# Linear attention and a maxout FFN on one core: a PSUM bank for each pair's small products, a late stage for left queries, and new numbers for the order

## The chip, the cores and the metric

The kernel runs on one core of a Trainium2 chip. The metric is device time in microseconds, from the first to the last instruction with what lies around them; before the change it is 717.27 us, the median of three runs (717.15 to 717.32).

## The reference

Attention without a softmax over scores: q is normalized by exp over the head dimension, k over the sequence, and `kv` is a 64 x 64 matrix per head. Its output x, 4608 rows of 512, goes through a maxout layer of three weights and a last product.

```python
batch, n_heads, seq, head_dim = 8, 8, 576, 64      # fp32
q_s = exp(q - max(q, -1));  q_s = q_s / (sum(q_s, -1) + 1e-9)
k_s = exp(k - max(k, 2));   k_s = k_s / (sum(k_s, 2) + 1e-9)
kv = einsum('bhsd,bhse->bhde', k_s, v)
x = einsum('bhsd,bhde->bhse', q_s, kv)             # to (4608, 512)
h = maximum(maximum(x @ w1, x @ w2), x @ w3)       # 512 -> 768
out = h @ w_out                                    # 768 -> 512
```

## The kernel before

**Tiles.** Two heads form a pair, so a batch has four pairs and the kernel 32 of them, numbered n = 4 b + g. The 576 rows of a head are 512 main rows and 64 left rows. The main rows of a batch are one chunk of the FFN; the left rows of all eight batches, 8 x 64 = 512, are a ninth, last chunk. x lies with its features on partitions, in `xbuf` for main rows and in `left` for left ones.

**FFN.** Each fp32 operand is split into a high and a low part in fp32r, and each product is three matmuls (low x high, high x low, high x high). A chunk has 18 gate groups of 12 matmuls (`gate`, L693) and 4 groups y of 18 (`second`, L732), all 128 x 512: 288 a chunk, 2592 in all. They are called main products here, and they accumulate in the four banks of the PSUM pool `pf`. Their weights are made on the core in 24 slices (18 of w1 to w3, 6 of w_out): a slice is loaded into a buffer `wst`, its words are joined in `wx` (L342 to L355), and it is split into `wh` and `wl`, or `oh` and `ol` (L363, L370). Buffers are few (`ROOMS`), and the loads wait for them on SP.

**Attention.** Batches 0 and 1 are "turned" (`TURNED = 2`), to fill the start. For such a pair PE transposes k (L441 the main rows, L445 the left rows), DVE takes the maximum over the sequence (L450 to L452), ACT the exp into `keT` (L456, L457), PE transposes it back (L464, L466), ten small matmuls form kv (L511), and ACT scales it into the block-diagonal `bdf` (L527). q is reduced on DVE (L550), goes through exp on ACT in ten pieces of 64 columns where `Q_BY_ACT` says so (L567), is scaled (L595), transposed on PE (L636, left L640), copied to `qf` (L645, L647) and multiplied with `bdf` in full fp32 (L663, once for 512 columns and once for 64). ACT and DVE split the result into `x`, or `left` (L666, L668). From batch 2 on, in the 24 "plain" pairs, q and k are not transposed by PE; the x product is three fp32r matmuls for the 512 main columns and, some products later, three for the 64 left ones.

**PSUM.** Eight banks: four of `pf`, three of `pa` for what is 512 wide, and one, `ps`, for everything small of all pairs. Its four quarters are handed out in turn (`next(small)`): left part of k, left part of keT, kv, left part of q, left x.

**What sets the order.** The order on every engine is written by a planner (`Streams`) while the program is built: each step has a cost, events it waits for, rooms in pools that it takes and frees, and a rank. Ranks come from numbers: `AT` and `STEP` for the eight turned pairs, `FIRST` and `CHUNK` for the plain ones, `SLICES_AT`, `SLICE` and `SLICE_STEP` for weight slices, `GATES_AT` for main products, and the string `FIRST_LOADS` for the loads of batch 0 on SP (lower case main rows, upper case left rows, w a weight slice). On the chip an engine runs its rows in that order and waits in place.

```python
quarters = ps.tile([P, 4, P], F32, name="ps")
small = (quarters[:, i % 4, :] for i in itertools.count())
```

Of the kernel before, what the change touches and what calls it, by code (L numbers as in the profile page):

```python
# [37 lines left out]
SLICES_AT, SLICE_STEP, SLICE_HI, SLICE_LO = -30.5, 2.83, 6.78, 0.26  # L38
GATES_AT = 50.0
FIRST_LOADS = 'qwQKkKqvVvwQkkwqVkwqvv'  # L40
ROOMS = 3, 2, 3, 4

Q_BY_ACT = (0, 1, 2, 3, 4, 5, 6)
# [6 lines left out]
def dve_reduce(n):  # L50
    return (n + 140) / 960
# [28 lines left out]
class Streams:  # L80
# [88 lines left out]
    def issue(self, t, e, c, s):  # L169
        step = s[4]  # L170
        end = t + c
# [24 lines left out]
def linear_attention_then_maxout_ffn(  # L196
# [26 lines left out]
    nc = tc.nc  # L223
# [22 lines left out]
    pa = ctx.enter_context(tc.tile_pool(name="pa", bufs=3, space=PSUM))  # L246
    ps = ctx.enter_context(tc.tile_pool(name="ps", bufs=1, space=PSUM))
# [16 lines left out]
    q0 = early.tile([P, H, 5, D], F32, name="q0")  # L264
    v0 = early.tile([P, H, 5, D], F32, name="v0")
    bdf = [start.tile([P, P], F32, name=f"bdf{i}", bufs=1) for i in range(2)]
    qbuf = [start.tile([P, 2, 5, D], F32, name=f"q1{i}", bufs=1) for i in range(2)]
# [14 lines left out]
    nc.gpsimd.memset(q0[LEFT:P, :, 4, :], 0.0)  # L282
    for i in range(2):
        nc.gpsimd.memset(bdf[i], 0.0)
    for i in range(2):
        nc.gpsimd.memset(qbuf[i][LEFT:P, :, 4, :], 0.0)
        nc.gpsimd.memset(vbuf[i][:, :, :, D:NV], 1.0)
        nc.gpsimd.memset(vbuf[i][LEFT:P, :, 4, :], 0.0)
# [13 lines left out]
    st = Streams({"pf": 4, "pa": 3, "ps": 4, "keT": 1, "hp": NJ, "tmp": 3, "ke": 2, "qe": 2, "qf": 1, "qt": 2, "tb": 1, "qT": 2, "qhl": 1}, {"pf": in_pf})  # L302
    late_pools, turn_pools = [], []

    quarters = ps.tile([P, 4, P], F32, name="ps")
    small = (quarters[:, i % 4, :] for i in itertools.count())
# [67 lines left out]
    class Pair:  # L374


        def __init__(self, b, g):
            self.b, self.g = b, g
            self.hs = slice(2 * g, 2 * g + 2)
            self.n = b * NP + g  # L380
            self.m = self.n % 2
            self.turned = b < TURNED
            if b == 0:
                self.kt, self.vt, self.qt = k0[:, :, self.hs], v0[:, self.hs], q0[:, self.hs]
            else:
                self.kt, self.vt = kbuf[self.m], vbuf[self.m]
                if self.turned:
                    self.kt = self.kt.rearrange("p h s d -> p (h s d)").rearrange("p (s h d) -> p s h d", s=5, h=2)

        def ago(self, what, *u):  # L390

            return (what, self.n - 2, *u) if self.n >= 2 else None

# [15 lines left out]
        def v_load(self):  # L409
            if self.b:  # L410
                prev = self.ago("kv") if self.n >= NP + 2 else None
                for hh in range(2):
                    yield Step("S", 0.64, [prev], kb=200)
                    nc.sync.dma_start(out=self.vt[:, hh, 0:4, 0:D], in_=head_rows(v, self.b, 2 * self.g + hh))
# [3 lines left out]
        def q_load(self):  # L418
            if self.b == 0:
                return  # L420
            if self.turned:
                prev = self.ago("qsub") if self.n >= NP + 2 else None
                self.qt = qbuf[self.m]
                yield Step("S", 0.64, [prev], kb=256)
                nc.sync.dma_start(out=self.qt[:, :, 0:4, :], in_=main_rows(q, self.b, self.hs))
                yield Step("S", 0.64, gives=("q", self.n), kb=50)
                nc.sync.dma_start(out=self.qt[0:LEFT, :, 4, :], in_=left_rows(q, self.b, self.hs))
# [6 lines left out]
        def k_turned(self):  # L434

            n, kt = self.n, self.kt
            rooms = [("pa", ("kT", n)), ("ps", ("kTl", n))]
# [6 lines left out]
            kTl = next(small)  # L444
            nc.tensor.transpose(  # L445
                out=kTl[:, :LEFT], in_=kt[:LEFT, 4].rearrange("p h d -> p (h d)"), identity=ident[:LEFT, :LEFT]
            )
            yield Step("V", dve_reduce(CH) + dve_reduce(LEFT) + 0.13)
            km = att.tile([P, 2], F32, name="km2", bufs=4)
            nc.vector.tensor_reduce(out=km[:, 0:1], in_=kT, op=ALU.max, axis=AX.X, negate=True)  # L450
            nc.vector.tensor_reduce(out=km[:, 1:2], in_=kTl[:, :LEFT], op=ALU.max, axis=AX.X, negate=True)
            nc.vector.tensor_tensor(out=km[:, 0:1], in0=km[:, 0:1], in1=km[:, 1:2], op=ALU.min)  # L452
            yield Step("A", act(CH) + act(LEFT) + 0.2, free=rooms)
            keT = start.tile([P, S], F32, name="keT", bufs=1)
            ks = self.ks = att.tile([P, 2], F32, name="ks", bufs=4)
            nc.scalar.activation(out=keT[:, :CH], in_=kT, func=AF.Exp, bias=km[:, 0:1], accum_out=ks[:, 0:1])  # L456
            nc.scalar.activation(  # L457
                out=keT[:, CH:], in_=kTl[:, :LEFT], func=AF.Exp, bias=km[:, 0:1], accum_out=ks[:, 1:2]
            )
            rooms = [("pa", ("ke", n)), ("ps", ("kel", n))]  # L460
            yield Step("T", 0.6, take=rooms + [("ke", n)], free=[("keT", n)])
            kep = pa.tile([P, CH], F32, name="pa")
            for s in range(4):
                nc.tensor.transpose(out=kep[:, s * P : (s + 1) * P], in_=keT[:, s * P : (s + 1) * P], identity=ident)  # L464
            kel = next(small)
            nc.tensor.transpose(out=kel[:LEFT, :], in_=keT[:, CH:], identity=ident)  # L466
            e = yield Step("AV", (act(CH) + act(P), dve(CH) + dve(P)), free=rooms)
            ke = self.ke = att.tile([P, 5, 2, D], F32, name="ke")
            for o, i in (
                (ke[:, 0:4].rearrange("p s h d -> p (s h d)"), kep),  # L470
                (ke[:LEFT, 4].rearrange("p h d -> p (h d)"), kel[:LEFT, :]),
            ):
                (nc.scalar.copy if e == "A" else nc.vector.tensor_copy)(out=o, in_=i)
# [24 lines left out]
        def k_steps(self):  # L498
# [3 lines left out]
            last = [("ps", ("kv", n))]  # L502
            yield Step(
                "T", 0.9, [("v", n), self.ago("xmm", 0), self.ago("xmm", 1)], take=last, free=[("ke", n)], gives=("kv", n)
            )
            kv = next(small)
# [17 lines left out]
            yield Step("A", 0.65, free=last if turned else (), gives=("bd", n) if turned else None)  # L524
            for r in heads:
                to = (bdf if turned else bdh)[self.m]
                nc.scalar.activation(out=to[r, r], in_=kv[r, 0:D], func=AF.Copy, scale=rk[r])  # L527
            if not turned:
                yield Step("V", 0.45, free=last, gives=("bd", n))
# [11 lines left out]
        def q_steps(self):  # L541
            n = self.n
            rows = 10 if self.turned else QS
            by_act = n in Q_BY_ACT
            qm = att.tile([P, rows], F32, name=f"qm{rows}", bufs=4)
            qs = att.tile([P, rows], F32, name=f"qs{rows}", bufs=4)
            yield Step("V", dve_reduce(rows * D), [("q", n)])
            if self.turned:
# [4 lines left out]
                if by_act:  # L553
                    yield Step("A", 5 * 0.33, take=[("qe", n)])
# [4 lines left out]
                qe = self.qe = start.tile([P, 5, 2, D], F32, name="qe", bufs=2)  # L559
                rows3 = qe.rearrange("p s h d -> p (s h) d")  # L560
                sums = qs.rearrange("p (s h) -> p s h", h=2)
                if by_act:
                    for hh in range(2):
                        if hh:
                            yield Step("A", 5 * 0.33, gives=("qsub", n))
                        for s in range(5):
                            nc.scalar.activation(  # L567
                                out=qe[:, s, hh, :], in_=src[:, hh, s, :], func=AF.Exp,
                                bias=qm[:, 5 * hh + s : 5 * hh + s + 1], accum_out=sums[:, s, hh : hh + 1],
                            )  # L570
                else:
# [3 lines left out]
                        in1=qm.rearrange("p (h s) -> p h s", h=2).unsqueeze(3).broadcast_to([P, 2, 5, D]),  # L575
                        op=ALU.subtract,
                    )
            else:
# [5 lines left out]
                )  # L584
            if not by_act:
# [4 lines left out]
            yield Step("V", 0.34)  # L590
# [34 lines left out]
        def x_place(self, u):  # L625
            if u == 0:
                return tuple(xbuf[self.b % 2][:, i, self.g, :] for i in range(2))
            return tuple(left[:, i, self.g, self.b * LEFT : (self.b + 1) * LEFT] for i in range(2))

        def turned_steps(self):  # L630

            n = self.n
            yield Step("T", 0.5, [("qn", n)], take=[("qf", n), ("pa", ("qT", n)), ("ps", ("qTl", n))], free=[("qe", n)])
            qT = pa.tile([P, CH], F32, name="pa")
            for s in range(4):
# [3 lines left out]
            qTl = next(small)  # L639
            nc.tensor.transpose(  # L640
                out=qTl[:, :LEFT], in_=self.qe[:LEFT, 4].rearrange("p h d -> p (h d)"), identity=ident[:LEFT, :LEFT]
            )
            e = yield Step("AV", (act(CH), dve(CH)), free=[("pa", ("qT", n))])
            qf = start.tile([P, S], F32, name="qf", bufs=1)
            (nc.scalar.copy if e == "A" else nc.vector.tensor_copy)(out=qf[:, :CH], in_=qT)  # L645
            yield Step("A", act(LEFT), free=[("ps", ("qTl", n))], gives=("qhl", n))
            nc.scalar.copy(out=qf[:, CH:], in_=qTl[:, :LEFT])  # L647
            self.terms = [(bdf[self.m], qf)]

        def x_steps(self, u):  # L650
            n, b = self.n, self.b
            cs = (slice(0, CH), slice(CH, S))[u]
            w = cs.stop - cs.start
            room = ("ps" if u else "pa", ("x", u, n))
            cost = f32(w) if self.turned else 3 * f32r(w)
            after = [("bd", n), ("qhl", n), ("xmm", n, 0) if u else None]
            if u == 0:
                after += [("gates", b - 2) if b >= 2 else None, "late" if b == 1 else None]
            yield Step("T", cost, after, take=[room], gives=("xmm", n, u), free=[("qf" if self.turned else "qhl", n)] if u else ())
            xT = (next(small) if u else pa.tile([P, CH], F32, name="pa"))[:, :w]  # L660
            last = len(self.terms) - 1
            for i, (l, r) in enumerate(self.terms):
                nc.tensor.matmul(out=xT, lhsT=l, rhs=r[:, cs], start=(i == 0), stop=(i == last))  # L663
            h, lo = self.x_place(u)
            yield Step("A", act(w))
            nc.scalar.copy(out=h, in_=xT)  # L666
# [257 lines left out]
```

## Time and profile before

| | us |
|---|---|
| median of three runs | 717.27 |
| the profiled execution | 717.27 |
| its span | 715.5 |
| PE busy | 685.4 |
| DVE busy | 401.7 |
| ACT busy | 254.0 |
| GpSimd busy | 55.1 |

How to read the lines of the profile: `L663 PE MATMUL pa<-qf,bdf` is line 663 of the kernel on TensorE, what it writes, and from what. A row of the timeline starts with its start and its length in us; `x2` counts instructions merged into the row; brackets hold the idle time of the engine before it and what ended it. A row of the waits reads: who waited, for whom, us in total, how often, the longest. A group of instructions gives its count, busy time and mean in ns, then the idle time before. PE's ends are modelled, and its instructions overlap, so the pace of a series is read from the starts. The program's fp32 matmuls appear as two rows each.

### The profile page before, as it was taken

How to read it: one execution, taken by the hardware profiler on the slowest of the kernel's cores; microseconds unless marked ns; L12 is line 12 of the kernel's file. 1: busy time of each engine (PE TensorE's matmuls, PEld its weight loads, DVE VectorE, ACT ScalarE, POOL GpSimd, SP SyncE). 2: the span in 40 equal slices, each digit the busy share in tenths (PEclk: the TensorE clock that was granted, in tenths of full speed). 3: DMA queues.
4: the chain of work that ended last, by engine and by line, in shares of the span. 5: the costliest groups of instructions: out<-in, count | busy, mean ns of one | idle time of the engine just before them, and what ended most of it. 6: DMA issues, size and time to landing. Idle time of an engine off the chain costs nothing.

```text
span 715.5 us, 9842 instructions
## 1 busy us (share of the span) xinstructions
PE 685.4 (96%) x3528; PEld 552.0 (77%) x3528; DVE 401.7 (56%) x812; ACT 254.0 (36%) x605; POOL 55.1 (8%) x69
## 2 busy tenths in 40 slices
PE   3779899999999999999999999999999999999997
PEld 2457687787888787888888888888888888888885
DVE  6789867388977977865477646653422112211220
ACT  4899745433443425422442234223411111111111
POOL 1222233100010000000000000000000000000000
PEclk9999999999999999999999999999999999999999
DMA  8947423315454334520253015200200010010002
GB/s 222 252 135 231 127 83 106 109 34 129 113 163 122 83 80 110 151 65 17 73 150 86 16 49 164 64 16 28 82 1 0 16 45 0 1 44 16 1 0 60
DMA packets 86417, 58.07 MB, mean 81 GB/s; under 512 B 53344, under 2 KB 77920, under 8 KB 86368
## 3 DMA queue, kind: packets, MB, share of 16 engines
q1 hardware_dynamic: 86288, 57.31, 28.9%
q8 instruction: 28, 0.46, 0.3%
q14 instruction: 21, 0.17, 0.1%
q10 hardware_dynamic: 80, 0.13, 0.0%
HBM read 40.89 MB, written 9.44 MB: 70 GB/s over the span
## 4 chain that ended last, share of the span: by engine, by line
PE 88%; ACT 4%; DVE 4%; DMA 2%; issue 1%; SPq 1%; DVEq 0%; ACTq 0%
PE pf L693 59%; PE pf L732 21%; PE ps L511 3%; PE pa L663 2%; ACT qe L567 2%; PE ps L663 1%; DMA wst<-in_moe_w_dram 1%; ACT keT L456 1%; ACT wst L359 0%; PE pa L464 0%; DMA v<-in_v_dram 0%; DVE m L705 0%; DVE wx L346 0%; PE pa L441 0%; DMA vt<-in_v_dram 0%
## 5 line engine op out<-in xcount | busy, mean ns | idle before, releaser
L693 PE MATMUL pf<-x,wh 128*128 128x512 f32 x1152 | 357.3, 391 | 0.0
L693 PEld LDWEIGHTS pf<-x,wh 128*128 128x128 f32 x1152 | 217.3, 189 | 47.0 <-issue 1.0
L693 PE MATMUL pf<-x,wl 128*128 128x512 f32 x576 | 231.1, 401 | 0.0
L705 DVE TENSOR_TENSOR m<-pf,m 128x512 f32<-128x512 f32 x108 | 74.4, 689 | 180.0 <-PE pf L693 177.5
L693 PEld LDWEIGHTS pf<-x,wl 128*128 128x128 f32 x576 | 108.7, 189 | 23.9 <-issue 0.7
L708 ACT CAST h_h<-m 128x512 fp32r<-128x512 f32 x54 | 33.6, 622 | 191.6 <-DVE m L705 191.4
L732 PE MATMUL pf<-ol,h_h 128*128 128x512 f32 x216 | 88.0, 408 | 0.1
L732 PE MATMUL pf<-oh,h_l 128*128 128x512 f32 x216 | 84.5, 391 | 0.0
L732 PE MATMUL pf<-oh,h_h 128*128 128x512 f32 x216 | 84.3, 390 | 0.0
L702 ACT COPY m<-pf 128x512 f32<-128x512 f32 x54 | 31.7, 587 | 57.8 <-PE pf L693 57.7
L732 PEld LDWEIGHTS pf<-ol,h_h 128*128 128x128 f32 x216 | 40.6, 188 | 9.2 <-DVE ol L370 0.7
L712 DVE TENSOR_TENSOR h_l<-m,h_h 128x512 fp32r<-128x512 f32 x54 | 36.9, 683 | 19.1 <-ACT h_h L708 19.0
L732 PEld LDWEIGHTS pf<-oh,h_l 128*128 128x128 f32 x216 | 40.5, 188 | 9.1
L732 PEld LDWEIGHTS pf<-oh,h_h 128*128 128x128 f32 x216 | 40.6, 188 | 7.6
L693 PE MATMUL pf<-left,wh 128*128 128x512 f32 x144 | 44.4, 389 | 0.0
L486 POOL PARTITION_ALL_REDUCE kma<-km x24 | 18.7, 779 | 299.7 <-DVE ke L489 146.8
L750 ACT COPY m<-pf 128x512 f32<-128x512 f32 x35 | 20.4, 587 | 59.8 <-PE pf L732 54.3
L355 POOL TENSOR_TENSOR wst<-wx,wst 128x512 int32<-128x512 int32 x24 | 31.6, 1318 | 90.9 <-DVE wx L351 55.5
L668 DVE TENSOR_TENSOR x<-pa,x 128x512 fp32r<-128x512 f32 x32 | 22.1, 689 | 29.4 <-ACT x L666 29.3
L600 DVE STREAM_TRANSPOSE tb<-qt 128x576 f32<-128x576 f32 x24 | 30.8, 1282 | 2.4 <-DMA qT<-tb 2.1
L666 ACT CAST x<-pa 128x512 fp32r<-128x512 f32 x32 | 18.7, 585 | 36.1 <-PE pa L663 36.1
L693 PEld LDWEIGHTS pf<-left,wh 128*128 128x128 f32 x144 | 27.0, 188 | 5.7
(114 smaller groups left out, 679.2 us busy)
## 6 DMA issues: line engine op xcount, KB each, us to landing
wst<-in_moe_w_dram SPq DMA_DIRECT2D x18, 512.0 KB, 5.0
out_dram<-m SPq DMA_DIRECT2D x32, 256.0 KB, 2.4
vt<-in_v_dram SPq DMA_DIRECT2D x56, 128.0 KB, 3.0
qt<-in_q_dram SPq DMA_DIRECT2D x24, 288.0 KB, 3.1
qT<-tb SPq DMA_DIRECT2D x192, 36.0 KB, 1.9
kt<-in_k_dram SPq DMA_DIRECT2D x24, 256.0 KB, 3.0
wst<-in_moe_w_out_dram SPq DMA_DIRECT2D x6, 512.0 KB, 3.3
q<-in_q_dram SPq DMA_DIRECT2D x8, 256.0 KB, 4.6
```

The source lines that it names most:

```text
L355: nc.gpsimd.tensor_add(out=low.bitcast(I32), in0=x.bitcast(I32), in1=low.bitcast(I32))
L511: nc.tensor.matmul(out=kv[r, :nv], lhsT=ke[rows, s, hh, :], rhs=self.vt[rows, hh, s, 0:nv], start=(s == 0), stop=(s == 4),)
L600: nc.vector.transpose(out=tb.rearrange("p e (c s) -> p s e c", s=QS), in_=self.qt.rearrange("p s (e c) -> p s e c", e=2))
L663: nc.tensor.matmul(out=xT, lhsT=l, rhs=r[:, cs], start=(i == 0), stop=(i == last))
L668: nc.vector.tensor_sub(out=lo, in0=xT, in1=h.bitcast(F32))
L693: nc.tensor.matmul(out=ps, lhsT=l[:, cc, js], rhs=r, start=(cc == 0 and t == 0), stop=(cc == NC - 1 and t == 2))
L702: nc.scalar.copy(out=m, in_=self.m.pop((j, 0)))
L705: nc.vector.tensor_max(out=m, in0=self.m.pop((j, i)), in1=m)
L708: nc.scalar.copy(out=h, in_=m)
L712: unit[e].tensor_sub(out=lo, in0=m, in1=h.bitcast(F32))
L732: nc.tensor.matmul(out=po, lhsT=l, rhs=r[:, j, :], start=(j == 0 and i == 0), stop=(j == NJ - 1 and i == 2))
L750: nc.scalar.copy(out=o, in_=po)
```

## The change

**A bank per pair.** The bank `ps` is gone. A pair's small products now lie in one bank that the pair takes for itself: left k in the first quarter, left keT in the second, kv in the third, a new sum of q in the fourth. The four pairs of batch 0 take their banks from `pf`, ahead of the first gate group; later pairs share a new pool `sm` with one bank (`BANKS = 3, 1`), held from the pair's first small product to its last.

**Left queries.** The 64 left rows of q of batches 0 and 1 are left out of the turned pairs, whose q is now 512 wide (`q0`, `q1`, `qe` with 4 instead of 5 parts). A stage `left_queries` does both batches at once after the turned part: two loads, six rows on DVE, exp and two copies on ACT, four transposes and eight products of 64 columns on PE. For it `bdf` keeps the matrices of all eight turned pairs.

**Left products.** In the plain pairs the three 64-column products stand between the three 512-column ones, in one step.

**Two kinds of q.** `Q_BY_ACT` now names pairs 0 and 3 to 7: eight pieces each. Pair 2 goes through one wide exp. Pair 1 (`Q_AFTER`) too, and isn't scaled before its product: with q transposed as weights, PE forms x in rows and the sums of q beside it (`of_head`, a matrix of ones per head), DVE divides, and PE transposes x back.

**Order.** All numbers of the order are replaced, and the planner takes PE's costs 1.85 times as high before 34 us of its own clock (`COLD`).

```diff
-FIRST, CHUNK, SLICE = 21.0, 39.5, 0.35
-AT = (16.0, 6.9, 25.7, 26.2, 99.1, 87.2, 114.2, 74.5)
-STEP = (0.38, 3.02)
-GATES_AT = 50.0
-FIRST_LOADS = 'qwQKkKqvVvwQkkwqVkwqvv'
+COLD = 34.0, 1.85
+FIRST, CHUNK, SLICE = 143.0, 39.5, 1.32
+AT = (38.7, -49.7, 32.6, 13.7, 143.7, 146.4, 163.0, 85.8)
+STEP = (7.87, 0.38)
+GATES_AT = 1000.0
+FIRST_LOADS = 'vkwkKqvwKVwVqqkwvqkv'
+BANKS = 3, 1
-Q_BY_ACT = (0, 1, 2, 3, 4, 5, 6)
+Q_BY_ACT = (0, 3, 4, 5, 6, 7)
+Q_AFTER = (1,)
...
-    ps = ctx.enter_context(tc.tile_pool(name="ps", bufs=1, space=PSUM))
+    sm = ctx.enter_context(tc.tile_pool(name="sm", bufs=BANKS[1], space=PSUM))
...
-    in_pf = []
+    in_pf = [("sm", n) for n in range(NP)]
...
+        def small_room(self):
+            return ("pf", ("sm", self.n)) if self.b == 0 else ("sm", self.n)
+        def take_small(self):
+            self.sm = (pf if self.b == 0 else sm).tile([P, CH], F32, name="pf" if self.b == 0 else "sm")
...
-            yield Step("T", 0.6, [("k", n)], take=rooms + [("keT", n)], gives=("ksub", n))
-            kT = pa.tile([P, CH], F32, name="pa")
+            yield Step("T", 0.6, [("k", n)], take=[*room, ("keT", n), self.small_room()], gives=("ksub", n))
+            self.take_small()
+            kT, kTl = pa.tile([P, CH], F32, name="pa"), self.sm[:, 0:LEFT]
...
-            kv = next(small)
+            if not turned:
+                self.take_small()
+            kv = self.sm[:, 2 * P : 3 * P]
...
-                        for s in range(5):
+                        for s in range(4):
                             nc.scalar.activation(
...
+            if self.after:
+                yield Step("A", act(rows * D), gives=("qn", n))
+                nc.scalar.activation(out=rows3, in_=rows3, func=AF.Exp)
+                return
...
+            for s in range(4):
+                l = qf[:, s * P : (s + 1) * P]
+                nc.tensor.matmul(out=sums[:, 2 * s : 2 * s + 2], lhsT=l, rhs=of_head, start=True, stop=True)
+                nc.tensor.matmul(out=xn[:, s * P : (s + 1) * P], lhsT=l, rhs=bdf[:, n], start=True, stop=True)
...
-            for i, (l, r) in enumerate(self.terms):
-                nc.tensor.matmul(out=xT, lhsT=l, rhs=r[:, cs], start=(i == 0), stop=(i == last))
+                parts = [(xT, slice(0, CH))] + ([] if self.turned else [(self.sm[:, 0:LEFT], slice(CH, S))])
+                last = len(self.terms) - 1
+                for i, (l, r) in enumerate(self.terms):
+                    for out, cs in parts:
+                        nc.tensor.matmul(out=out, lhsT=l, rhs=r[:, cs], start=(i == 0), stop=(i == last))
...
+            yield Step("V", dve(LEFT), free=[self.small_room()], gives=("xl", b, self.g))
+            nc.vector.tensor_sub(out=lo, in0=self.sm[:, 0:LEFT], in1=h.bitcast(F32))
+    def left_queries():
...
+        for g in range(NP):
             nc.tensor.transpose(
+                out=qTp[:, g * P : (g + 1) * P], in_=ql[:, 2 * g : 2 * g + 2].rearrange("p r d -> p (r d)"), identity=ident
             )
...
+        for n in range(TURNED * NP):
+            b, g = divmod(n, NP)
+            at = g * P + b * LEFT
+            nc.tensor.matmul(out=xT[:, at : at + LEFT], lhsT=bdf[:, n], rhs=qT[:, at : at + LEFT], start=True, stop=True)
```

Three places of the order, before and after. The first is ACT between the third and the fourth x of batch 0 (`CAST x`). Before:

```order
L666 CAST x_86<-pa 128x512
L666 CAST left<-ps 128x64
L527 ACTIVATE bdf_101<-ps,rk 64x64 x2
L456 ACTIVATE keT,ks<-pa,km_603 128x512
L457 ACTIVATE keT,ks<-ps,km_603 128x64
L645 COPY qf<-pa 128x512
L359 ACTIVATE wst<-wst 128x512
L342 ACTIVATE wx<-wst 128x512
L363 CAST wh_80<-wx 128x4x128
L647 COPY qf<-ps 128x64
L567 ACTIVATE qe,qs_144<-q_103,qm_143 128x64 x5
L359 ACTIVATE wst<-wst 128x512
```

And now:

```order
L693 CAST x_86<-pa 128x512
L466 ACTIVATE keT,ks<-pa,km_559 128x512
L467 ACTIVATE keT,ks<-sm,km_559 128x64
L649 COPY qf<-pa 128x512
L535 ACTIVATE bdf<-pf,rk 64x64 x2
L367 CAST wh_80<-wx 128x4x128
L363 ACTIVATE wst<-wst 128x512
L576 ACTIVATE qe,qs_138<-q_101,qm_137 128x64 x4
L693 CAST x_86<-pa 128x512
```

The copies of left columns are gone from between, and four instead of five pieces of exp (those of a pair of batch 1) stand ahead of the fourth x. From the program's start to that x, ACT has 112 rows before, with 50 such pieces, and 79 now, with 20.

The second place is PE around the last x product of batch 0. Before it stands among other turned steps, ahead of main product 34 to 36:

```order
L466 MATMUL ps<-ident,keT 64x128
L693 MATMUL pf<-x_86,wl_82 128x512
L693 MATMUL pf<-x_86,wh_79 128x512 x2
L693 MATMUL pf<-x_86,wl_83 128x512
L693 MATMUL pf<-x_86,wh_80 128x512 x2
L693 MATMUL pf<-x_86,wl_84 128x512
L693 MATMUL pf<-x_86,wh_81 128x512 x2
L663 MATMUL pa<-qf,bdf_101 128x512
```

Now it stands behind main product 21:

```order
L645 MATMUL pa<-ident,qe 128x128 x4
L472 MATMUL pa<-ident,keT 128x128 x4
L473 MATMUL sm<-ident,keT 64x128
L775 MATMUL pf<-x_86,wl_82 128x512
L775 MATMUL pf<-x_86,wh_79 128x512 x2
L690 MATMUL pa<-qf,bdf 128x512
L519 MATMUL sm<-vt_92,ke 64x64 x10
L775 MATMUL pf<-x_86,wl_82 128x512
```

Behind it the turned steps of batch 1 stand one by one among 12 to 33 main products, and the last turned x product has 261 main products ahead of it; before, the last one has 315, and its left part 321, and nine turned products and transposes of batch 1 stand in one row behind main product 96.

The third place is PE in a plain pair (b = 2). Before, six main products lie between the x product and its left part, and kv of the next pair follows after six more:

```order
L663 MATMUL pa<-q_l,bdh_1505 128x512
L663 MATMUL pa<-q_h,bdl_1509 128x512
L663 MATMUL pa<-q_h,bdh_1505 128x512
L693 MATMUL pf<-x_765,wl_84 128x512
L693 MATMUL pf<-x_765,wh_81 128x512 x2
L693 MATMUL pf<-x_765,wl_82 128x512
L693 MATMUL pf<-x_765,wh_79 128x512 x2
L663 MATMUL ps<-q_l,bdh_1505 128x64
L663 MATMUL ps<-q_h,bdl_1509 128x64
L663 MATMUL ps<-q_h,bdh_1505 128x64
```

Now the left products alternate with the others, and kv (L519) follows after 18 main products:

```order
L690 MATMUL pa<-q_l,bdh_1378 128x512
L690 MATMUL sm<-q_l,bdh_1378 128x64
L690 MATMUL pa<-q_h,bdl_1382 128x512
L690 MATMUL sm<-q_h,bdl_1382 128x64
L690 MATMUL pa<-q_h,bdh_1378 128x512
L690 MATMUL sm<-q_h,bdh_1378 128x64
L775 MATMUL pf<-x_665,wl_84 128x512
L775 MATMUL pf<-x_665,wh_81 128x512 x2
```

More of the change, by code (lines that the diff above doesn't have):

```diff
@@ L1 @@
-import itertools
 from contextlib import ExitStack
@@ L170, in issue @@
         step = s[4]
+        if e == "T" and t < COLD[0]:
+            c *= COLD[1]
         end = t + c
@@ L281, in linear_attention_then_maxout_ffn @@
         )
[L282 to L288, printed above, removed]
+    nc.gpsimd.memset(of_head, 0.0)
+    for h, r in enumerate(heads):
+        nc.gpsimd.memset(of_head[r, h : h + 1], 1.0)
+    nc.gpsimd.memset(bdf, 0.0)
     def main_rows(src, b, hs):
@@ L501, in k_steps @@
             ke = self.ke
-            last = [("ps", ("kv", n))]
+            after = turned and n in Q_AFTER
             yield Step(
-                "T", 0.9, [("v", n), self.ago("xmm", 0), self.ago("xmm", 1)], take=last, free=[("ke", n)], gives=("kv", n)
-            )
-            kv = next(small)
+                "T", 0.9, [("v", n), None if turned else self.ago("xmm")], take=() if turned else [self.small_room()],
+                free=[("ke", n)], gives=("kv", n),
+            )
+            if not turned:
+                self.take_small()
+            kv = self.sm[:, 2 * P : 3 * P]
             nv = D if turned else NV
@@ L523, in k_steps @@
             nc.vector.reciprocal(out=rk, in_=rk)
-            yield Step("A", 0.65, free=last if turned else (), gives=("bd", n) if turned else None)
+            yield Step("A", 0.65, free=[self.small_room()] if turned and not after else (), gives=("bd", n) if turned else None)
             for r in heads:
-                to = (bdf if turned else bdh)[self.m]
+                to = bdf[:, n] if turned else bdh[self.m]
                 nc.scalar.activation(out=to[r, r], in_=kv[r, 0:D], func=AF.Copy, scale=rk[r])
             if not turned:
-                yield Step("V", 0.45, free=last, gives=("bd", n))
+                yield Step("V", 0.45, gives=("bd", n))
                 for r in heads:
@@ L542, in q_steps @@
             n = self.n
-            rows = 10 if self.turned else QS
+            rows = 8 if self.turned else QS
             by_act = n in Q_BY_ACT
+            self.after = self.turned and n in Q_AFTER
             qm = att.tile([P, rows], F32, name=f"qm{rows}", bufs=4)
@@ L623, in q_steps @@
             self.terms = [(bdh[self.m], q_l), (bdl[self.m], q_h), (bdh[self.m], q_h)]
[L625 to L628, printed above, removed]
         def turned_steps(self):
             n = self.n
-            yield Step("T", 0.5, [("qn", n)], take=[("qf", n), ("pa", ("qT", n)), ("ps", ("qTl", n))], free=[("qe", n)])
+            room = [("pa", ("qT", n))]
+            yield Step("T", 0.5, [("qn", n)], take=[("qf", n), *room], free=[("qe", n)])
             qT = pa.tile([P, CH], F32, name="pa")
@@ L638, in turned_steps @@
                 )
-            qTl = next(small)
+            e = yield Step("AV", (act(CH), dve(CH)), free=room, gives=None if self.after else ("qhl", n))
+            (nc.scalar.copy if e == "A" else nc.vector.tensor_copy)(out=qf, in_=qT)
+            if not self.after:
+                self.terms = [(bdf[:, n], qf)]
+                return
+            room = [("pa", ("xn", n))]
+            yield Step("T", 1.2, [("bd", n)], take=room, free=[("qf", n)])
+            xn, sums = pa.tile([P, CH], F32, name="pa"), self.sm[:, 3 * P : 4 * P]
@@ L646, in turned_steps @@
[L646 to L661, printed above, removed]
-            for i, (l, r) in enumerate(self.terms):
[L663 to L666, printed above, removed]
-            yield Step("V", dve(w), free=[room], gives=("x", b, self.g) if u == 0 else ("xl", b, self.g))
-            nc.vector.tensor_sub(out=lo, in0=xT, in1=h.bitcast(F32))
@@ L672, in linear_attention_then_maxout_ffn @@
+        xv = xT.rearrange("p (g t) -> p g t", g=NP)
+        h, lo = (left[:, i, :, 0 : TURNED * LEFT] for i in range(2))
+        yield Step("A", act(CH))
+        nc.scalar.copy(out=h, in_=xv)
+        yield Step("V", dve(CH), free=room, gives="left")
+        nc.vector.tensor_sub(out=lo, in0=xv, in1=h.bitcast(F32))
     class Chunk:
@@ L682, in gate @@
             for cc in range(NC):
-                x = [("x", c, cc)] if c < B else [("xl", b, cc) for b in range(B)]
+                x = [("x", c, cc)] if c < B else ["left", *(("xl", b, cc) for b in range(TURNED, B))]
                 yield Step(
@@ L805, in open_late @@
     def open_late():
-        yield Step("-", 0.0, [(x, 0, g) for x in ("x", "xl") for g in range(NP)], gives="late")
+        yield Step("-", 0.0, [("x", 0, g) for g in range(NP)], gives="late")
         early_stack.close()
@@ L818, in open_turn @@
     def open_turn():
-        yield Step("-", 0.0, [("split", n) for n in range(NS)] + [("xl", 1, g) for g in range(NP)], gives="turn")
+        yield Step("-", 0.0, [("split", n) for n in range(NS)] + [("x", 1, g) for g in range(NP)], gives="turn")
         start_stack.close()
@@ L878, in linear_attention_then_maxout_ffn @@
             st.add(p.turned_steps(), at + 5 * step, step)
-        for u in range(2):
-            st.add(p.x_steps(u), -500.0 + at / 100 + u if b else at + 6 * step + u * 0.1)
+        st.add(p.x_steps(), -500.0 + at / 100 if b else at + 6 * step)
+    st.add(left_queries(), FIRST + CHUNK * 4)
     for c, ch in enumerate(chunks):
```

147 lines of the change are left out of this document (102 added, 45 removed).

## The prediction

> **What bounds the kernel now.** I read the head of the page first, then the slices, then busy time by stage.
>
> ```profile
> span 715.5 us, 9842 instructions
> PE 685.4 (96%) x3528; PEld 552.0 (77%) x3528; DVE 401.7 (56%) x812; ACT 254.0 (36%) x605; POOL 55.1 (8%) x69
> PE   3779899999999999999999999999999999999997
> ```
>
> TensorE is busy in all slices but the first four or five, some 18 us each: what can be gained quickly lies in the first 80 us. The profiled execution took 717.27 us, which is also the median of the three runs; its span is 715.5, so 1.77 us lie outside. I work in times of the span and add 1.77 at the end.
>
> ```profile
> 0.00:33.10 33.10, 15.72 (x84) 10.69 (x85) 22.89 (x59) 21.75 (x91) 7.26 (x17) 1.00 0.97 241
> 33.10:58.00 24.90, 20.73 (x125) 14.85 (x123) 21.54 (x53) 23.08 (x87) 6.50 (x5) 1.00 0.43 128
> 58.00:82.40 24.40, 21.39 (x130) 16.51 (x130) 22.93 (x51) 19.58 (x61) 5.78 (x6) 0.97 0.70 209
> 82.40:110.70 28.30, 28.30 (x122) 23.40 (x122) 19.65 (x37) 17.03 (x39) 9.10 (x8) 0.97 0.29 92
> ```
>
> Columns: stretch, length, then busy time of PE, weight loads, VectorE (DVE), ScalarE (ACT), GpSimd. From 33 to 58 us ACT is busy 23.1 of 24.9 us, to 82 us DVE 22.9 of 24.4; from 82.4 on PE has no hole. So the start is set by the two elementwise engines, and the rest by PE's own work. The waits of PE say in what form the start costs it:
>
> ```profile
> PE ps L511 <- DVE km L451: 2.5, 2, 1.5
> PE ps L663 <- ACT keT L457: 1.6, 1, 1.6
> PE ps L640 <- ACT keT L457: 1.4, 1, 1.4
> PE ps L511 <- ACT keT L457: 1.4, 1, 1.4
> PE ps L640 <- DVE left L668: 1.2, 1, 1.2
> PE ps L511 <- ACT qf L647: 1.0, 1, 1.0
> PE ps L445 <- ACT ke L473: 0.7, 1, 0.7
> PE ps L663 <- DVE km L451: 0.6, 1, 0.6
> ```
>
> Each is a product into `ps` that waits for another engine which reads the `ps` of a different product, mostly of another pair: all small products share one bank. Together 10.4 us of idle PE, all before 82 us. Two further places matter: the last x product of batch 0 with the DVE row that ends it, and the end of the turned batches.
>
> ```profile
> 55.05 1.02 PE L663 MATMUL pa<-qf,bdf 128*128 128x512 f32 x2
> 57.29 0.69 DVE L668 TENSOR_TENSOR x<-pa,x 128x512 fp32r<-128x512 f32 x1 [0.37 <-ACT x L666]
> 103.16 1.28 DVE L370 TENSOR_TENSOR wl<-wst,wh 128x512 fp32r<-128x512 f32 x2
> 127.26 0.68 DVE L370 TENSOR_TENSOR ol<-wst,oh 128x512 fp32r<-128x512 f32 x1
> 143.47 13.35 PE pf L693 x57
> ```
>
> Batch 0 is complete at 57.98 (57.29 + 0.69). The 18 slices of the gate weights are split at 104.44, the last of w_out at 127.94. The last turned product ends at 143.47; by the order 321 main products have run then. What follows, 572.0 us to the end, is 2271 main products and 24 plain pairs.
>
> **The start: elementwise work.** Counted in the two orders up to the row that ends the fourth x of batch 0, ACT has 112 rows before and 79 after, with the same 8 weight casts, 5 `keT`, 4 x and 8 `bdf`.
>
> ```profile
> 47.42 0.33 ACT L567 ACTIVATE qe<-q,qm 128x64 f32<-128x64 f32 x1
> L666 ACT CAST left<-ps 128x64 fp32r<-128x64 f32 x32 | 6.8, 214 | 17.3 <-PE ps L663 13.7 <-DVE wx L347 2.2 <-PE ps L511 1.4
> L342 ACT ACTIVATE wx<-wst 128x512 f32<-128x512 f32 x13 | 8.5, 662 | 0.0
> ```
>
> The pieces of exp fall from 50 to 20: 30 x 0.33 = 9.9 us. Seven 64-column copies go (7 x 0.21 = 1.5) and one 512-wide copy of a weight (0.66). Added are two exps over 512, one copy and two weight rows, 5 x 0.6 = 3.0. ACT is relieved by 9.1 us.
>
> ```profile
> L595 DVE TENSOR_TENSOR qe<-qe,qs 128x640 f32<-128x640 f32 x8 | 6.6, 820 | 0.1
> L550 DVE TENSOR_REDUCE qm<-q 128x10 f32<-128x640 f32 x8 | 6.4, 809 | 0.0
> L344 DVE TENSOR_SCALAR wx<-wst 128x512 uint32<-128x512 uint32 x11 | 4.5, 410 | 2.9 <-DMA wst<-in_moe_w_dram 2.8
> ```
>
> On DVE three rows of L344 go (1.2), three left subtractions (0.22 each: 0.7), one split that POOL takes and one copy (0.69 each: 1.4); four q rows over 640 become 512 (4 x 0.13 = 0.5) and six maxima too (0.8); one sum over 512 is added (0.7). DVE is relieved by 3.9 us. So the fourth x comes between 57.98 - 9.1 = 48.9 and, with DVE as dense as now, 54.1. Against it speaks the new order of loads: the first q is seventh, behind some 1570 KB instead of first, 3 us later at the 241 GB/s of the first row. DVE, with the larger sum, is the nearer end: I take **53.7**, and for its PE product 2.9 us earlier as now (57.98 - 55.05), 50.8.
>
> **From there to main product 321.** Two bounds. PE: from that product on the new order interleaves main products with every turned step, so PE should run without a hole. 21 main products are done then (33 now), 300 are left.
>
> ```profile
> 370.82 45.10 PE pf L693 x198
> 113.44 0.88 PE ps L511 x20
> 117.26 0.45 PE pa L464 x4
> 124.33 0.86 PE pa L663 x2
> 125.89 0.17 PE ps L663 x2
> 132.04 0.44 PE pa L636 x4
> 132.47 0.20 PE ps L640
> ```
>
> 300 x 0.228 (45.10 / 198) = 68.3. Turned steps left: 5 x products (0.86), 4 kv (0.88), 3 k transposes (0.44 + 0.20), 3 of keT (0.45 + 0.10), 4 of q (0.44): 13.1. That gives 50.8 + 81.4 = 132.2. Supply: now the 18th split comes 46.5 us after batch 0 (104.44 - 57.98), the last of w_out 23.5 later. Behind it the new order needs the last 12 products of y and 33 gates, 45 x 0.228 = 10.3. Kept at that pace: 53.7 + 46.5 + 23.5 + 10.3 = **134.0**, so the supply of weights binds, not PE. I add 1.0 for in-order waits of the new start: 135.0 against 143.47, a gain of 8.5. That the eight turned left products (0.17) and transposes (0.20) left this stretch is in it. Ends: 130 if the slices come with ACT's 9 us (48.9), 139.2 if the 18th split stays at 104.44 (104.44 + 33.8 + 1.0).
>
> **The late left stage.** Its elementwise rows lie beside main products, and only the last chunk reads what they make; were that cover gone, six DVE rows of about 0.69 (the row at 57.29) would cost 4 us. On PE: 4 transposes and 8 products of 64 columns, 0.44 + 8 x 0.17 = **1.8 added** (between 1.3, at 0.11 each as below, and 2.6, at the 0.27 that one `ps` L663 of the start takes).
>
> **Left products beside the main ones,** 24 pairs.
>
> ```profile
> 182.70 0.25 PE ps L663 x3
> 182.68 0.28 PE L663 MATMUL ps<-q_h,bdh 128*128 128x64 f32 x1
> 182.79 0.48 PE L693 MATMUL pf<-x,wl 128*128 128x512 f32 x1
> 183.10 0.62 PE L693 MATMUL pf<-x,wh 128*128 128x512 f32 x2
> ```
>
> Three left products take 0.25, the last 0.11 (182.68 to 182.79), and the 512-wide product behind them takes 0.31 instead of 0.23. Hidden beside the main ones they would save 24 x 0.25 = 6.0; if each of the three 512-wide products behind one pays 0.08 (one does now), they cost 24 x 0.16 = 3.8. The spacing of 0.11 is the same whether a 64- or a 512-wide product follows, so it stays: **0**.
>
> [...]
>
> **One bank for the plain pairs.** The new pool `sm` has a single bank from batch 1 on, so kv of the next pair waits until the left subtraction of this one has read it.
>
> ```profile
> 142.00:212.00 70.00, 70.00 (x408) 56.35 (x407) 59.92 (x129) 28.51 (x55) 6.73 (x8) 1.00 0.39 104
> ...
> 180.63 0.69 PE pa L663 x3
> ...
> 185.27 0.23 DVE L668 TENSOR_TENSOR left<-ps,left 128x64 fp32r<-128x64 f32 x1
> ```
>
> Now that subtraction ends 4.9 us behind the start of the x product, on a DVE that is 86% busy (59.92 of 70). The new order puts 18 main products in between: 18 x 0.228 + 0.69 + 0.25 = 5.0. The left product comes 6 main products (1.4 us) earlier, so about 1.5 us are spare. Behind a kv that waits stand all main products. From 0 (covered) to 0.5 a pair, 11.5; nearest to the row is covered, I take **1.0** in all. The other banks moved (`pf` lends four to batch 0 before any gate opens there) cost nothing while the first gate has to wait for x anyway.
>
> Sum: 715.5 - 8.5 + 1.8 + 0 + 1.0 = 709.8, and 711.6 with the 1.77 outside.
>
> **Rivals.**
> - The slices don't come earlier (chance 0.16). Their loads queue on SP for buffers, and those counts are unchanged; against it, the wait for a buffer is a wait for splits, which DVE now does sooner. 139.2 instead of 135.0: 715.8.
> - The single bank makes PE wait (0.10). For it: DVE is near full there, and PE takes orders in turn. Against it: the spare 1.5 us. At 0.5 us in each of 23 pairs it adds 10.5 to the sum, 722; it turns the result to slower from 0.3 us a pair on.
> - The bank waits don't go: in batch 1 one `sm` bank again couples pairs, and each pair's own chain (k, exp, kv) still waits on itself (0.07). Then the start keeps its 143.5, and with 1.8 added and the 3.0 us of turned left work (8 x 0.37) gone: 716.
> - The left products do hide (0.06): 711.6 - 6.0 = 705.6.
> - My forecast 0.61, between 707.5 (130 at main product 321) and 714 (138 there).
>
> The range of 8 in 10 takes in the first two ends and half of the slow ones: 706.5 to 717. A measurement here tells about 0.2% from no change, 715.8 to 718.7. Faster: forecast, hidden products and over half of the first and third rival, 0.78; within 0.2%: the rest of these, 0.12; slower 0.10.
>
> **What would show it.** Right: the fourth x of batch 0 ends on DVE at 52 to 55; the table of PE's waits loses the rows on `ps` above; no hole and no drop of clock between 75 and 85; the last turned x product stands before main product 262, at about 120; the 18th split near 100; 0.11 between left product and the next. Wrong: kv rows L519 waiting for the left subtraction; the 18th split still at 104; ACT or DVE idle on q or weight loads between 10 and 33 us, so that x comes at 58 again.

## The result, and the profile after

| | before | after |
|---|---|---|
| median of six runs, us | 717.30 | 712.03 |
| lowest to highest | 716.95 to 719.56 | 710.43 to 714.59 |
| span of the profiled execution | 715.5 | 711.8 |
| fourth x of batch 0 complete on DVE | 57.98 | 59.50 |
| main product 321 ends | 143.47 | 139.65 |
| from there to the end of the span | 572.0 | 572.15 |

The ratio is 0.9925, with a 95% interval of 0.9906 to 0.9944. The forecast was 711.6. The total is right; two of its terms are not, and they offset each other, so that it came out this close is luck. The profiled execution of after took 713.57, 1.5 above the median, so its span stands a little high beside the table. Two executions of the experiments lay far above the rest at a lower granted clock (765.79 us at 0.85 with the left rows of v behind, 1132.58 at 0.566 with one bank), and the medians and ratios below leave them out.

The busy slices of PE in after:

```profile
PE   3579999999999999999999999999999999999997
```

Three stretches of the prediction's second fence, now in after (PE, weight loads, DVE, ACT, GpSimd, then the granted clock, the DMA share and GB/s):

```profile
33.10:58.00 24.90, 17.96 (x111) 13.69 (x112) 17.37 (x42) 17.21 (x55) 5.18 (x4) 0.79 0.50 156
58.00:82.40 24.40, 24.40 (x132) 19.45 (x131) 22.20 (x48) 23.40 (x76) 8.49 (x7) 1.00 0.77 230
82.40:110.70 28.30, 28.30 (x166) 22.64 (x165) 24.46 (x48) 17.15 (x39) 8.27 (x7) 1.00 0.38 112
```

From 58 us on PE has no pause left; before, it was idle 3.0 us up to 82. Ahead of 58 the start is emptier than it was. ACT falls from 23.1 to 17.2 of 24.9 us, as it should, but DVE falls from 21.5 to 17.4 as well, and PE from 20.7 to 18.0. Nobody is the bound there: all three wait. The waits say for what. PE over the whole span, then the two elementwise engines up to 75 us, in after:

```profile
PE pf L658 <- ACT qf L649: 6.5, 1, 6.5
```

```profile
ACT wst L363 <- DMA wst<-in_moe_w_dram: 19.1, 6, 6.5
DVE wx L348 <- DMA wst<-in_moe_w_dram: 12.0, 4, 6.0
```

The same two engines before:

```profile
ACT wst L359 <- DMA wst<-in_moe_w_dram: 6.7, 4, 4.5
...
DVE wx L344 <- DMA wst<-in_moe_w_dram: 2.8, 1, 2.8
```

All `ps` rows of the prediction are gone, as forecast. ACT and DVE now wait 31.1 us for slices of the weights instead of 9.5, and PE waits for ACT. Why the slices are late stands in the queue of loads, SP's own waits up to 50 us and its timeline in after:

```profile
SPq L429 <- DMA vt<-in_v_dram: 8.0, 2, 4.0
```

```profile
23.47 0.81 SPq L427 DMA_DIRECT2D vt<-in_v_dram  x1
28.36 0.63 SPq L429 DMA_DIRECT2D vt<-in_v_dram  x1
...
31.09 0.67 SPq L336 DMA_DIRECT2D wst<-in_moe_w_dram  x1
...
32.35 1.90 SPq L427 DMA_DIRECT2D vt<-in_v_dram  x2
38.39 0.62 SPq L429 DMA_DIRECT2D vt<-in_v_dram  x1
39.11 1.09 SPq L336 DMA_DIRECT2D wst<-in_moe_w_dram  x2
```

Twice SP stands still ahead of L429, the load of the left rows of v: from 24.28 (23.47 + 0.81) to 28.36, and from 34.25 to 38.39, 4.1 us each. Everything behind it on SP waits too. There are three buffers, so the fifth slice goes where the second lay and the sixth where the third lay. DVE split these two early:

```profile
18.14 0.68 DVE L374 TENSOR_TENSOR wl<-wst,wh 128x512 fp32r<-128x512 f32 x1
...
23.35 0.69 DVE L374 TENSOR_TENSOR wl<-wst,wh 128x512 fp32r<-128x512 f32 x1
```

So the buffers were free at 18.82 and 24.04; the slices went out at 31.09 and 39.11.

The cause is a part of the change that the section on it does not name. For batch 1, v is now packed without the column of ones:

```diff
+                    self.vt = self.vt.rearrange("p h s d -> p (h s d)")[:, : 10 * D]
+                    self.vt = self.vt.rearrange("p (h s d) -> p h s d", h=2, s=5)
```

The left rows of head 0 then lie between the main rows of the two heads. No byte is shared, but the stretch from the first to the last byte of the left rows spans the main rows of head 1, and the program gives L429 a wait for the landing of the load just ahead of it. These are SP's rows with the waits that the program gives them at that place, in after and with the left rows laid behind (the experiment below); DMAHW5 counts the landing of the load just ahead:

```
after   L427 DMA vt0_92<-in_v_dram 128x256 [waits DMAHW5_49]
        L429 DMA vt0_92<-in_v_dram 64x2x64 [waits DMAHW6_49,DMAHW5_49]
behind  L427 DMA vt0_92<-in_v_dram 128x256 [waits DMAHW5_49]
        L429 DMA vt0_92<-in_v_dram 64x2x64 [waits DMAHW6_49]
```

That such a stretch alone draws the wait is not shown. In the kernel before, the left rows lie between the main rows as well, only unpacked, with a column of ones behind each row of 64, and there the left load goes out right behind the main ones (23.54 + 1.28 = 24.82):

```profile
23.54 1.28 SPq L414 DMA_DIRECT2D vt<-in_v_dram  x2
24.99 0.62 SPq L416 DMA_DIRECT2D vt<-in_v_dram  x1
```

So in after SP stands still 4.1 us each time for the landing of bytes that do not meet those of the load behind it.

Where the prediction's other places stand in after: the fourth x (PE, DVE), the 18th gate split and the last split of w_out, in the timelines of PE and of DVE:

```profile
56.38 1.02 PE L690 MATMUL pa<-qf,bdf 128*128 128x512 f32 x2
```

```profile
58.82 0.68 DVE L695 TENSOR_TENSOR x<-pa,x 128x512 fp32r<-128x512 f32 x1
...
102.50 0.68 DVE L374 TENSOR_TENSOR wl<-wst,wh 128x512 fp32r<-128x512 f32 x1
...
127.76 0.69 DVE L374 TENSOR_TENSOR ol<-wst,oh 128x512 fp32r<-128x512 f32 x1 [0.46 <-POOL wst L359]
```

The last turned x and the run of main products with number 321 in it, in the chain of after:

```profile
125.09 0.86 PE pa L690 x2
...
132.10 9.61 PE pf L775 x42
```

Number 321 is the 33rd of those 42: 132.10 + 33 x 0.2288 = 139.65.

### The profile page after: what moved, and what is told of

Same layout as the page of the kernel before. It is cut to its first block, busy times and chain, and to the rows that moved or that the text cites. A ratio compares the mean times of both kernels' runs of the same rounds, so it can differ in the third digit from the quotient of the medians.

```text
span 711.8 us, 9805 instructions
## 1 busy us (share of the span) xinstructions
PE 681.8 (96%) x3542; PEld 553.5 (78%) x3542; DVE 400.0 (56%) x804; ACT 245.0 (34%) x554; POOL 56.3 (8%) x71
## 4 chain that ended last, share of the span: by engine, by line
PE 92%; DMA 3%; SPq 2%; DVE 1%; ACT 0%; issue 0%; ACTq 0%; DVEq 0%
PE pf L775 63%; PE pf L814 21%; PE pa L690 4%; DMA wst<-in_moe_w_dram 3%; PE sm L519 3%; SPq L870 0%; SPq L413 0%; PE sm L690 0%; PE pa L645 0%; PE pa L453 0%; PE pa L744 0%; SPq L873 0%; DVE qm L559 0%; DVE wl L374 0%; PE pa L472 0%
```

## The experiments

Each ratio is to the kernel before on the same chip; its median there was 717.8, 717.8 and 717.1 in the three groups.

| run | median us | ratio, interval |
|---|---|---|
| after, again | 711.43 | 0.9913, 0.9897 to 0.9928 |
| after, left rows of v behind | 705.89 | 0.9831, 0.9809 to 0.9853 |
| the same, again | 705.92 | 0.9833, 0.9814 to 0.9852 |
| after, products apart | 711.62 | 0.9911, 0.9893 to 0.9929 |
| before, v packed | 721.89 | 1.0055, 1.0037 to 1.0073 |
| left rows behind, one bank | 705.10 | 0.9821, 0.9805 to 0.9837 |
| left rows behind, old numbers | 711.88 | 0.9915, 0.9898 to 0.9931 |
| old numbers, one bank | 712.32 | 0.9932, 0.9909 to 0.9954 |
| old numbers, more exp | 725.39 | 1.0119, 1.0092 to 1.0145 |

**The reference.** 

> The changed kernel again, as the reference for the runs beside it. Every theory expects what it gave before: about 712 us, fourth x of batch 0 complete on DVE near 59.5 us, ACT waiting about 19 us for weight slices in the first 75 us.

It gave 711.43, with the fourth x at 58.49 and 18.5 us of ACT's waits on slices.

**The wait in the queue of loads.** One load is placed elsewhere, and kv reads the left rows there; every row of every engine keeps its place.

```diff
+                    self.vl, self.vt = self.vt[:, 8 * D :].rearrange("p (h d) -> p h d", h=2), self.vt[:, : 8 * D].rearrange("p (h s d) -> p h s d", h=2, s=4)
...
-                nc.sync.dma_start(out=self.vt[0:LEFT, :, 4, 0:D], in_=left_rows(v, self.b, self.hs))
+                nc.sync.dma_start(out=self.vl[0:LEFT] if self.turned else self.vt[0:LEFT, :, 4, 0:D], in_=left_rows(v, self.b, self.hs))
```

> The changed kernel, but in the packed v buffers of batch 1 the left rows of both heads lie behind the main rows of both heads, not between them; the order of all instructions stays word for word. Theory A (a wait in the queue of loads): in the changed kernel the load of the left rows of v waits until the load just ahead of it has landed, 4.1 us at 24.3 and again at 34.3, and two weight slices stand queued behind it. Then the fifth slice goes out near 27 instead of 31.1, the sixth near 32 instead of 39.1, ACT waits about 10 us less for slices, the fourth x of batch 0 is complete at 52 to 55 instead of 59.5, and the time falls by 3 to 5 us, to 707 to 709. Rival B (the new order of loads itself): the batch 1 loads stand ahead of the slices and take the queue and the DMA engines whatever waits; the fifth slice still comes after 29, x after 58, the time within 1 us of 712.

SP's timeline of this run at the same place:

```profile
22.53 0.64 SPq L427 DMA_DIRECT2D vt<-in_v_dram  x1
23.21 0.63 SPq L429 DMA_DIRECT2D vt<-in_v_dram  x1
...
26.06 0.54 SPq L336 DMA_DIRECT2D wst<-in_moe_w_dram  x1
...
28.91 1.21 SPq L336 DMA_DIRECT2D wst<-in_moe_w_dram  x2
```

Its waits for slices up to 75 us, its second stretch, its fourth x, and the run of main products that holds number 321, from its chain:

```profile
ACT wst L363 <- DMA wst<-in_moe_w_dram: 11.4, 6, 6.1
DVE wx L348 <- DMA wst<-in_moe_w_dram: 6.4, 4, 4.0
```

```profile
33.10:58.00 24.90, 24.24 (x141) 18.83 (x141) 22.14 (x53) 22.49 (x74) 8.83 (x7) 0.87 0.53 158
```

```profile
51.29 0.69 DVE L695 TENSOR_TENSOR x<-pa,x 128x512 fp32r<-128x512 f32 x1
```

```profile
124.68 9.61 PE pf L775 x42
```

SP's table of waits up to 50 us has no row of L429 left. The fifth slice goes out 5.0 us earlier than in the profile above, the sixth 10.2; DVE is at 22.1 of 24.9 us instead of 17.4; the fourth x is complete at 51.98 instead of 58.49 beside it. These 6.5 us arrive whole at the end of the two profiled executions, whose span falls from 711.0 to 704.5; the medians differ by 5.5. Theory A stands and rival B falls, though the effect was a little larger than expected (707 to 709) and ACT's waits fell by 7.1 us instead of 10. This version takes 705.9, 1.7% less than the kernel before.

**The same part of the change alone, on the kernel before.** 

> The kernel before, with one part of the change alone: v of batch 1 packed without the column of ones, so that its left load waits for the landing of the load ahead (the settings of ones and zeros move to the end of the turned batches). Theory A: the same stall of 3 to 4 us appears twice in the queue of loads, at about 24 and 30 us, and slices behind it come as much later; as ACT is the nearer limit in this start (23 of 25 us busy), only part of it shows: 1 to 4 us slower than 717.3. Rival B: packing only makes the loads shorter, 0 to 1 us faster.

SP's timeline of this run, and its fourth x on DVE:

```profile
24.10 1.14 SPq L414 DMA_DIRECT2D vt<-in_v_dram  x2
28.46 0.61 SPq L416 DMA_DIRECT2D vt<-in_v_dram  x1
```

```profile
59.71 0.69 DVE L668 TENSOR_TENSOR x<-pa,x 128x512 fp32r<-128x512 f32 x1 [0.37 <-ACT x L666]
```

From 25.24 to 28.46, and again later, SP stands still here too. 721.89 against 717.76: 4.1 us, just above the 1 to 4 that theory A gave. Part of it only is seen at the fourth x (60.40 against 57.98); the 18th gate split comes 5.0 later (109.44 against 104.44). So packing with the left rows between costs time in both kernels. No run compares the packing with the left rows behind against v unpacked in the same kernel.

**Left products.** 

> The changed kernel, but in the 24 plain pairs the three 512-wide products run first and the three left products of 64 columns behind them, as before the change. My step: a left product costs its 0.11 us wherever it stands, so within 1 us of 712. Rival: beside the main ones they hide, so that apart they cost 24 x 0.16 to 24 x 0.25, 716 to 718.

```diff
-                for i, (l, r) in enumerate(self.terms):
-                    for out, cs in parts:
+                for out, cs in parts:
+                    for i, (l, r) in enumerate(self.terms):
```

711.62 against 711.43. PE's timeline of after shows why the place does not matter:

```profile
291.47 0.47 PE L690 MATMUL pa<-q_h,bdl 128*128 128x512 f32 x1
...
291.81 0.47 PE L690 MATMUL pa<-q_h,bdh 128*128 128x512 f32 x1
```

From one 512-wide product to the next it is 0.34 (291.47 to 291.81) instead of 0.23: the left product between them costs its 0.11.

**The bank per pair.** The version with the left rows of v behind, with batch 0 in one bank again. 

> The changed kernel with the left rows of v behind the main rows, a second time, as the reference for the two runs beside it: 705 to 707 us, fourth x of batch 0 complete near 52.0.

> The same, with the bank per pair undone for batch 0: the small products of its four pairs lie in one PSUM bank, two pairs in each half of it by turns; the order of all instructions stays. Theory C (as in my prediction: products wait for readers of other pairs in their bank, 10.4 us of idle PE before the change): rows of PE's table of waits name such pairs again, the fourth x comes 2 to 6 us later than 52.0, and the time rises as much, to 708 to 712. Rival D (in the new order the pairs stand far enough apart, and what waits on the bank would have waited for slices anyway): x within 1 us of 52.0, time within 1 us of 706.

```diff
+            if self.b == 0:
+                if not shared:
+                    shared.append(pf.tile([P, CH], F32, name="pf"))
+                self.sm = shared[0][:, 256 * self.m : 256 * (self.m + 1)]
```

A row of waits on another pair is back in PE's table, and yet the fourth x is at 51.17, against 51.60 in the reference beside it (50.91 + 0.69):

```profile
PE pf L524 <- DVE km L467: 2.8, 2, 2.5
```

```profile
50.49 0.68 DVE L700 TENSOR_TENSOR x<-pa,x 128x512 fp32r<-128x512 f32 x1
```

The 2.8 us are not added to the start: PE's wait for `bdf` ahead of an x product is 1.3 us here and 3.1 in the reference. 705.10 against 705.92, with intervals that overlap: the bank per pair of batch 0 is worth nothing in the new order. Rival D stands. The same under the old numbers: 

> The new structure with the old numbers of the order, and the four pairs of batch 0 again in one bank as in the run with one bank in the new order, where it cost nothing. Theory C, kept for the old order alone (there ACT has fewer pauses in which a wait on the bank could hide): fourth x 1 to 5 us after 49.3, time 713 to 717. Rival D (a product that waits for its bank would have waited for its own engine shortly after): within 1 us of 711.9.

712.32 against 711.88, on another chip, with ratios whose intervals overlap again. The fourth x came at 49.60 against 49.34. In both runs less shares the bank than in the kernel before, as the left queries and left x that also lay in `ps` are no longer there, and no run puts the bank per pair into that kernel.

**Structure and order apart.** 

> The new structure (bank per pair, left queries as one late stage, left products beside the main ones, left rows of v behind) with the old numbers of the order: ranks, first loads, which pairs' exponentials ACT takes, and pair 1 normalised before its product as the others. Theory E (as in my prediction: the start is set by elementwise work, and ACT has 9.1 and DVE 3.9 us less of it whatever the order): the fourth x is complete at 49 to 54, and the time is 705 to 711. Rival F (the gain lies in the new numbers, above all in main products placed where PE had holes): x at 56 or later, time 713 to 718.

```diff
+FIRST, CHUNK, SLICE = 21.0, 39.5, 0.35
+AT = (16.0, 6.9, 25.7, 26.2, 99.1, 87.2, 114.2, 74.5)
+STEP = (0.38, 3.02)
...
+FIRST_LOADS = 'qwKkKqvVvwkkwqVkwqvv'
+Q_BY_ACT = (0, 1, 2, 3, 4, 5, 6)
+Q_AFTER = ()
```

The left rows of v lie behind in this run too. The fourth x on DVE, three stretches, a row of PE's waits up to 90 us, and the run of main products with number 321 in it, the 21st of 60, all of this run:

```profile
48.65 0.69 DVE L695 TENSOR_TENSOR x<-pa,x 128x512 fp32r<-128x512 f32 x1 [0.75 <-ACT x L693]
```

```profile
58.00:82.40 24.40, 21.01 (x104) 16.75 (x103) 21.60 (x43) 13.72 (x27) 6.81 (x6) 0.94 0.41 129
82.40:110.70 28.30, 27.39 (x156) 21.48 (x156) 21.31 (x41) 17.60 (x48) 10.15 (x8) 0.99 0.37 113
110.70:142.00 31.30, 29.88 (x149) 22.51 (x148) 20.00 (x39) 13.80 (x28) 5.98 (x15) 1.00 0.28 84
```

```profile
PE pf L775 <- DVE wl L374: 4.3, 3, 2.3
```

```profile
131.89 13.99 PE pf L775 x60
```

x is complete at 49.34, 8.6 us earlier than before and 2.3 earlier than in the new order beside it (51.60): the structure alone does what the prediction's first step says. But PE is idle 3.4 + 0.9 + 1.4 = 5.7 us behind it, in large part for splits of the weights (4.3 us up to 90). The new numbers give up 2.3 us at x and close these holes. Main product 321 ends at 136.8 (131.89 + 21 x 0.233) with the old numbers and at 132.2 with the new ones, and from there on both take some 572.2. By the medians the new numbers are worth 6.0 (711.88 to 705.92), by the profiled executions 4.5 (709.0 against 704.5). Neither theory holds whole: x came as theory E says, but the time is just above its 711; rival F is wrong on x and on the time, but the numbers do gain as much as the structure, 6.0 beside 5.9. Which of the numbers does it was not taken apart.

**ACT's work put back.** Behind each exponential of ACT in batch 0 stands one more, whose result nobody reads:

```diff
+                            if self.b == 0:
+                                nc.scalar.activation(
+                                    out=idle_row, in_=src[:, hh, s, :], func=AF.Exp,
+                                    bias=qm[:, 4 * hh + s : 4 * hh + s + 1], accum_out=idle_sum,
+                                )
```

> The new structure with the old numbers of the order, and behind each of the 32 exponentials of 64 columns that ACT takes in batch 0 a second one whose result nobody reads: 32 x 0.33 = 10.6 us of ACT work put back. Theory E (ACT's relief is what the structure gains): the fourth x comes 6 to 10 us after 49.3, main products and all behind it later, time 716 to 719, which is that of the kernel before. Rival G (ACT's waits for slices cover the added work, and the structure gains by other things): less than 3 us at x, time below 714.

The added group of ACT and the fourth x on DVE in this run:

```profile
L583 ACT ACTIVATE idle_row<-q,qm 128x64 f32<-128x64 f32 x32 | 10.9, 341 | 0.0
```

```profile
58.12 0.69 DVE L702 TENSOR_TENSOR x<-pa,x 128x512 fp32r<-128x512 f32 x1 [0.81 <-ACT x L700]
```

10.9 us of ACT move x by 9.5, from 49.34 to 58.81, 0.8 behind the kernel before. Theory E stands for x, and rival G falls. The time missed what theory E gave: it rises by 13.5 instead of 4 to 7. Some 4 us of that fall behind main product 321, where PE waits for nothing in either run, and their cause stays open.

## Why the prediction was right, and where it was wrong

- **What bounds the start: right for the structure, wrong for the changed kernel.** With the old numbers ACT's work does set x, as the added exponentials show. In the changed kernel the queue of loads sets it.
- **Fourth x at 53.7, between 48.9 and 54.1: failed.** It came at 59.50. The step counted ACT's and DVE's rows and charged the new order of loads 3 us at the first q; it never priced the wait that packing v adds to SP, nor what is queued behind it. With that wait away x stands at 51.98, inside the bounds, and with the old numbers at 49.34, near the lower one. The 3 us do not follow from their own figures, since 1570 KB at 241 GB/s are 6.5; DVE took up the first q 1.6 us later than before (10.33 against 8.74). The sign named for being wrong, engines idle on loads so that x comes at 58 again, is what the profile showed; the longest of these waits ended at 37.05, behind the 10 to 33 us that I had given.
- **From PE's fourth x to main product 321: PE's bound held to 1.9 us, the choice between the two bounds was wrong.** PE runs without a hole; 300 main products and the turned steps took 83.3 (56.38 to 139.65), and 83.3 again with the wait away (48.95 to 132.23), against 81.4. "The supply of weights binds, not PE" was wrong by little: the splits took 69.0 us from batch 0 on (59.50 to 128.45) against 70.0, and PE did not wait for them. Main product 321 came at 139.65 instead of 135.0: 5.8 lost at x, less 1.2 won behind it. The 18th split at 103.18 and the last turned x product at 125.09 are late too, against "near 100" and "about 120".
- **The cross-pair waits.** They went, and no hole is left between 75 and 85. But the 10.4 us of PE read from that table were no price in the changed kernel: with one bank again the time stays. Whether they were one before is not shown. No term of the sum rested on them.
- **Left stage 1.8: a little small.** PE's timeline of after:

```profile
292.94 0.60 PE L732 MATMUL pa<-ident,qt 128*128 128x128 f32 x4
293.29 0.48 PE L775 MATMUL pf<-x,wl 128*128 128x512 f32 x1
...
296.14 1.90 PE L744 MATMUL pa<-qT,bdf 128*128 128x64 f32 x16
297.96 0.80 PE L519 MATMUL sm<-vt,ke 128*64 128x65 f32 x20
```

  The transposes hold PE 0.35 (292.94 to 293.29), the eight products 1.82: 2.2 in all.
- **Left products 0: right,** 0.11 each between the 512-wide products (0.34 less 0.23), and 711.62 us against 711.43 with them apart.
- **One bank for the plain pairs, 1.0: not paid.** From 142 us on after has no row of PE's waits, so the 18 main products between do cover it.
- **The rest, 572.0 + 2.8.** It took 572.15. Of the 2.65 too many, 1.0 is the bank wait, less 0.4 for the left stage; 0.9 is a wait of the kernel before that I had left in its 572.0 and that the change removes:

```profile
PE ps L663 <- DVE bdl L531: 0.9, 2, 0.6
```

  The last 1.1 is not assigned to anything. So +4.65 at the start and -2.65 behind it made 711.8 of the span forecast at 709.8.

In sum the change is three things. The structure gains 5.9, for which ACT's relief is the cause that the added exponentials support; the new numbers gain 6.0, where PE's holes close; laying the left rows of packed v between the main rows loses 5.5. The bank per pair in batch 0 and the place of the left products move nothing.

## What to carry to other kernels

Read the waits of the queue that issues the loads as closely as those of the engines: here one small load that twice waited 4.1 us for a landing held back the loads behind it on SP, and engines waited for slices that had not been sent; with the left rows behind, the time fell by 5.5 us. A table of waits on a shared bank says where an engine stood, not what it would gain; undo the sharing alone, or put it back alone, before it is given a price. When a relieved engine does not become faster, look at whether all engines are idle together, as here from 33 to 58 us, where the queue of loads had become the bound.

## What the runs showed of the hardware

In after, the clock granted to PE is 0.50 to 0.53 in three stretches of 5 us:

```profile
25.00:30.00 5.00, 3.43 (x10) 2.26 (x11) 3.87 (x11) 4.90 (x14) 1.29 (x1) 0.50 0.48 121
...
35.00:40.00 5.00, 1.75 (x8) 1.75 (x9) 2.91 (x6) 2.95 (x14) 0.00 (x0) 0.50 0.19 61
40.00:45.00 5.00, 5.00 (x22) 4.38 (x22) 1.73 (x9) 2.69 (x10) 1.28 (x1) 0.53 0.65 212
```

In the first two of them end waits of PE for ACT, of 3.4 us (L690 for `bdf`) and of 6.5 (L658). The clock is at 0.50 there, and from 40 to 45 us PE is busy throughout, with 22 rows at 0.53. Four transposes of k take 1.06 us there and 0.60 from 45 to 50 us, where the clock is at 1.00:

```profile
41.82 1.06 PE L453 MATMUL pa<-ident,k 128*128 128x128 f32 x4
...
48.24 0.60 PE L453 MATMUL pa<-ident,kt 128*128 128x128 f32 x4
```

So part of what the start loses stands in rows that PE shows as busy. With the left rows of v behind, the stretch from 25 to 30 has 1.00.

The length of the last pause alone does not tell the clock in these two runs. With the left rows of v behind, the two longest pauses of PE from 20 to 40 us are 2.3 us (ahead of L690 at 25.59) and 1.6 (ahead of L658). From 25 to 30 us the clock is at 1.00, and from 35 to 40 at 0.54, on a PE that is busy throughout:

```profile
32.19 0.38 PE L658 MATMUL pf<-of_head,qf 128*128 128x2 f32 x2 [1.63 <-ACT qf L649]
```

```profile
35.00:40.00 5.00, 5.00 (x19) 3.97 (x19) 4.21 (x13) 4.61 (x11) 0.83 (x2) 0.54 0.05 10
```

So the half clock cannot be put down to the late loads alone, and what set it here stays open.
